# Scores stored with the keys outside, the gates' exponential emitted later, and new stage slots ahead of the seven-product step

## The chip, the core and the metric

The kernel runs on one core of a Trainium2 chip. The time is the device time of one execution in microseconds (us). The engines of the core work in parallel and each runs its own instructions in order: PE (TensorE, matrix products), DVE (VectorE), ACT (ScalarE), POOL (GpSimd) and SP, which here only issues DMA transfers. ACT issues some DMA transfers too, in the same queue as its arithmetic, so an issue that has to wait holds up the arithmetic behind it.

## What is computed

Two branches over the same input x (2048 rows, 640 columns) are mixed by a gate per row, `g = sigmoid(sum(x * gate_w))`:

```python
a = einsum("bsd,ed->bse", x, dft_hid_re);  b = einsum("bsd,ed->bse", x, dft_hid_im)
A = einsum("ts,bse->bte", dft_seq_re, a) - einsum("ts,bse->bte", dft_seq_im, b)
q = einsum("nd,dhc->nhc", x, w_q)                       # 32 heads, two halves of 128
s1 = einsum("nhd,ed->nhe", q[..., :128], k1);  s2 = einsum("nhd,ed->nhe", q[..., 128:], k2)   # 16 keys each
# the two best keys of s1 and of s2, the two best of their four sums -> two experts of 256 per head
gate = softmax(top_s);  act = gelu(x . u[expert]);  B = sum(gate * act * v[expert])
out = g * A + (1 - g) * B
```

The part that matters here is the choice of the keys: for each of the 2048 rows there are 32 heads times two halves = 64 groups of 16 scores, and in each group the largest and the second largest score and their places are needed.

## The kernel before

**Products.** Every float32 operand is split into a high and a low part (`split`, L129 on ACT for the high part, L130 on POOL or DVE for the low part), and each product is made of three (`mm3`, L134 to L136). A 128x512 result stays in one of eight PSUM banks (`b0` to `b7`).

**Stages.** The sequence transform comes in pieces `n = 0 .. NPC-1`, one 128x512 block of the transform matrix each (`wf`, split into `WS`, three pieces ahead of PE). Sixteen pieces make a chunk of 512 output columns in banks 0 to 4; at the chunk's end ACT copies the five banks into the five slots of the stage tile `ST` (L253), DVE multiplies them by the gate row (`gate_piece`, L225), and ACT issues their stores to DRAM (`store_piece`, L232). The stage slots are handed out in turn, 0 to 4. From piece `N0` (31) to `N1` (71) PE alternates the pieces with the score products: `score_half(i, a)` makes the scores of rows tile `i` (of 16), half `a` of the 64 groups, in bank 5 or 6 in turn, and ACT copies them into the tile `sc` (L585); `sc` has two slots, so tile `i + 2` needs the slot of tile `i`. From piece `Q0` (80) a chunk pair is made with seven products in place of eight (units `a11`, `s1`, `a12`, ...): `quad_step`. Its results rest in the same `ST` slots: `c22` in slots 0 and 1, `c` in slots 2 and 3, `w` in slot 4. After the eight steps of `a11`, `q_post` copies bank 0 into `w` (L304) and banks 5 and 6 into `c` (L275). The first `a12` step adds its last product onto bank 0, so PE needs the copy into `w` first; banks 5 and 6 are next written by unit `s2`, 16 steps later.

**The choice of keys** (`topk`, DVE only, once per rows tile): the largest of each group (L598, a reduction over 16), a comparison of all 1024 scores with it (L600), a product with a table of places (L602), the largest of that (L604, a reduction over 16), a comparison of the table with that place (L607), the chosen score pushed far down (L609), and the first four again. `sc` and the work tile `ew` are stored `[64 groups, 16 keys]`, the keys inside. After four rows tiles, `gates(b)` forms the four sums and picks two on DVE, ACT takes an exponential (L624), and DVE makes the two gate factors (L640 to L647). `rows(b)` then issues, per rows tile, three transposing DMAs on SP (L659) into `rt`, and ACT or (for the last four tiles) POOL copies `rt` into the table `rows` (L667, L665; steps of 8 elements in the output). `experts()` compares these rows on DVE (L808 to L810), PE sums them (L836), ACT copies the sums out (L817) and issues their stores (`gd<-cd`, L823).

**Order.** The order on every engine is the order of the calls in the program; nothing moves them later. The background work (`topk`, `gates`, `rows`, `experts`) is a list of generators in `Pump`. After every `mm3` the pump is told 0.68 us, runs generators up to a share of that time, and counts down the functions given to `space`, each of which is called a stated number of pump microseconds after the one before it. `at(n, f)` calls `f` after piece `n`.

**DMA counters.** All DMAs of SP and ACT take one of eight completion counters (`DMAHW0` to `DMAHW7`) in turn, in program order across both queues. Before an issue, its engine waits for the DMA that had the same counter before, so an issue on ACT can wait for a transfer of SP's queue.

Of the kernel before, what the change touches and what calls it, by code (L numbers as in the profile page):

```python
# [8 lines left out]
F32 = mybir.dt.float32  # L9
# [88 lines left out]
def gated_mix_kernel(ctx: ExitStack, tc: tile.TileContext, xT, xn, dreT, dimT, wsre, wsim, wq, kT, uT, vv, gw, out):  # L98
# [25 lines left out]
    def stage():  # L124
        return ST[:, rotate("st", 5)]
# [110 lines left out]
    def seq_piece(n):  # L236
# [11 lines left out]
        for d in ((4, 0, 1, 2, 3) if n == NPC - 1 else range(KD)):  # L248
            ds = slice(d * P, (d + 1) * P)
            mm3(banks[d], X[s][:, 0, ds], X[s][:, 1, ds], h, l, s == 0, s == NT - 1)  # L250
            if s == NT - 1:
                staged[w * NC + c, d] = f = stage()
                nc.scalar.activation(f, banks[d], AF.Copy)  # L253
            run_bg(0.68)
# [47 lines left out]
    def q_post(n, what):  # L302
        if what == "a11":
            nc.scalar.activation(qres["w"], qrole["W"], AF.Copy)  # L304
            q_copy("c", "X")
        elif what == "s1":
# [65 lines left out]
    for q, n in ((0, NT), (1, 2 * NT), (2, 3 * NT), (3, 4 * NT), (6, Q0), (7, NPC)):  # L372
        at(n + (2 if q == 0 else -5 if q == 6 else -2 if q > 1 else -1), load_row, q)
        at(n + (7 if q == 0 else 0), gate_piece, q)
        at(n + (8 if q == 0 else 4 if q == 6 else 1), store_piece, q)

# [176 lines left out]
    for n in range(N0):  # L553
# [11 lines left out]
    pools.append(p2)  # L565
    SC = pa.tile([P, 2, HH, E], F32, name="sc", tag="A")
    EW = pa.tile([P, 2, HH, E], F16, name="ew", tag="B")
    eq, wtab = EW[:, 0], EW[:, 1]
    nc.gpsimd.iota(wtab, pattern=[[0, HH], [-1, E]], base=E, channel_multiplier=0,
                   allow_small_or_imprecise_dtypes=True)  # L570
# [3 lines left out]
    def score_half(i, a):  # L574
# [7 lines left out]
        for k in range(KD):  # L582
            mm3(ps, xh[:, k, :], xl[:, k, :], WH[:, k, c], WL[:, k, c], k == 0, k == KD - 1)
            run_bg(0.68)
        nc.scalar.activation(scs[i].rearrange("p h e -> p (h e)")[:, c], ps, AF.Copy)  # L585
        if a == 1:
            picks(i, scs.pop(i))

    def topk(i, sc):
# [5 lines left out]
        for s in range(2):  # L595
            m = mm[:, s, ib, :]
            r = rr[:, s, ib, :]
            nc.vector.tensor_reduce(m, sc, op=OP.max, axis=AX.X)  # L598
            yield 1.22
            nc.vector.tensor_tensor(eq, sc, m[:, :, None].to_broadcast([P, HH, E]), op=OP.is_equal)  # L600
            yield 1.31
            nc.vector.tensor_tensor(eq, eq, wtab, op=OP.mult)  # L602
            yield 1.0
            nc.vector.tensor_reduce(r, eq, op=OP.max, axis=AX.X)  # L604
            yield 1.22
            if s == 0:
                nc.vector.tensor_tensor(eq, wtab, r[:, :, None].to_broadcast([P, HH, E]), op=OP.is_equal)  # L607
                yield 1.22
                nc.vector.scalar_tensor_tensor(sc, eq, FAR, sc, op0=OP.mult, op1=OP.add)  # L609
                yield 1.44  # L610

    def gates(b):
# [10 lines left out]
        nc.vector.tensor_sub(c[:, 1], c[:, 1], c[:, 0])  # L623
        nc.scalar.activation(c[:, 2], c[:, 1], AF.Exp)  # L624
        yield 1.2
# [12 lines left out]
        yield 1.3  # L638

        nc.vector.tensor_scalar(c[:, 1], c[:, 2], 1.0, None, op0=OP.add)  # L640
        nc.vector.reciprocal(c[:, 0], c[:, 1])
# [6 lines left out]
        gated[b] = (rp, gs)  # L648
        yield 1.5

    def rows(b):
# [26 lines left out]
        for a in range(NB + 1):  # L678
            bg.space(lambda a=a: step(a), 16.0 if a == 0 and b == NT // NB - 1 else 5.0 if b == NT // NB - 1 else 8.0)
        yield 0.0  # L680
# [5 lines left out]
    def picks(i, sc):  # L686
        bg.add(done(i, topk(i, sc)))
        if i % NB == NB - 1:
            bg.add(gates(i // NB))
        elif i and i % NB == 0:  # L690
            bg.add(rows(i // NB - 1))
        if i == NT - 1:
            bg.add(rows(NT // NB - 1))

# [535 lines left out]
```

## Time and profile before

| what | value |
|---|---|
| median of three runs | 785.89 us (785.76 to 787.21) |
| the profiled execution: its own time, and its span | 786.74 us, 785.0 us |
| PE busy | 762.9 us (97% of the span) |
| DVE busy | 579.9 us (74%), nearly all the time from 190 to 440 us |
| ACT busy | 302.2 us (38%) |
| POOL busy | 342.2 us (44%) |
| pieces with scores (the score stage) | about 150 to 420 us |
| start of the seven-product step | about 459 us |

A row of the timeline gives the start, the length, the engine, the line and the tiles, and in brackets how long the engine stood idle before and what ended that. `ACTq` and `SPq` rows are DMA issues. A row of groups gives the count, the busy time, the mean length in ns, and the idle time ahead.

### The profile page before, as it was taken

Reading aid. Unit: us, or ns where it says so; the run is one execution under the profiler, and the core shown is the slowest. Engines: PE = TensorE matmul, PEld = TensorE weight load, DVE = VectorE, ACT = ScalarE, POOL = GpSimd, SP = SyncE. Lnnn points to the kernel's source line nnn. Section 1 sums busy time; section 2 is a strip of 40 time slices with the busy share of each in tenths; the row PEclk is TensorE's granted clock in tenths of the full one; section 3 lists DMA queues with packets and bytes.
Section 4 is the critical chain, followed back from the end, with each engine's and each line's share of the span. In section 5 each row is a group of like instructions: output and inputs, shape, how many; then the busy total and the mean of one; then the engine's idle time right before and its main releaser. Section 6 shows DMA issues by size and latency. Waiting matters only on the chain.

```text
span 785.0 us, 12383 instructions
## 1 busy us (share of the span) xinstructions
PE 762.9 (97%) x4568; PEld 612.4 (78%) x4568; DVE 579.9 (74%) x676; ACT 302.2 (38%) x505; POOL 342.2 (44%) x239
## 2 busy tenths in 40 slices
PE   9999999999999999998999996999999999999997
PEld 6777677888888788886888774877777887788886
DVE  7651121398999999999999984888888768748761
ACT  5344323322315243344334442444334442543351
POOL 4532224466756476476654042000002466567253
PEclk9999999999999999999999997999999999999999
DMA  9966986645445665456645487798857486676411
GB/s 343 375 247 187 300 336 220 213 155 194 144 167 165 213 197 205 156 158 220 228 146 183 161 244 230 230 292 267 271 149 235 154 292 218 198 257 216 127 61 68
DMA packets 115180, 165.29 MB, mean 211 GB/s; under 512 B 35760, under 2 KB 51248, under 8 KB 115120
## 3 DMA queue, kind: packets, MB, share of 16 engines
q1 hardware_dynamic: 85648, 144.69, 56.1%
q10 hardware_dynamic: 29472, 19.81, 8.0%
q8 instruction: 36, 0.59, 0.3%
q14 instruction: 24, 0.20, 0.1%
HBM read 126.17 MB, written 36.71 MB: 208 GB/s over the span
## 4 chain that ended last, share of the span: by engine, by line
PE 52%; DVE 27%; DMA 9%; POOL 4%; issue 3%; SPq 2%; ACT 2%; ACTq 0%; DVEq 0%; POOLq 0%
PE b L134 17%; PE b L135 16%; PE b L136 16%; DVE ew L600 3%; DVE rr L604 3%; DVE mm L598 3%; DVE ew L602 3%; POOL WS L130 2%; PE b L479 2%; DVE ew L607 2%; DMA wf<-in_wsim 2%; DVE ST L225 2%; DVE sc L609 2%; DVE WS L130 2%; DMA wq<-in_wq 1%
## 5 line engine op out<-in xcount | busy, mean ns | idle before, releaser
L134 PE MATMUL b<-WS,X 128*128 128x512 f32 x555 | 221.2, 399 | 10.8 <-ACT ST L304 7.5
L135 PE MATMUL b<-WS,X 128*128 128x512 f32 x555 | 217.9, 393 | 1.6 <-DVE WS L130 1.6
L136 PE MATMUL b<-WS,X 128*128 128x512 f32 x555 | 217.1, 391 | 0.0
L130 POOL TENSOR_TENSOR WS<-wf,WS 128x512 fp32r<-128x512 f32 x72 | 109.4, 1525 | 134.1 <-ACT WS L129 125.7
L134 PEld LDWEIGHTS b<-WS,X 128*128 128x128 f32 x555 | 104.8, 189 | 42.5 <-ACT ST L304 8.0
L129 ACT ACTIVATE WS<-wf 128x512 fp32r<-128x512 f32 x152 | 94.5, 632 | 95.1 <-PE b L136 41.1
L135 PEld LDWEIGHTS b<-WS,X 128*128 128x128 f32 x555 | 104.9, 189 | 23.9 <-DVE WS L130 3.4
L136 PEld LDWEIGHTS b<-WS,X 128*128 128x128 f32 x555 | 104.8, 189 | 22.5
L130 DVE TENSOR_TENSOR WS<-wf,WS 128x512 fp32r<-128x512 f32 x80 | 54.3, 702 | 27.0 <-ACT WS L129 26.9
L130 POOL TENSOR_TENSOR WS<-ra,WS 128x512 fp32r<-128x512 f32 x40 | 59.2, 1497 | 15.1 <-ACT WS L129 14.4
L585 ACT ACTIVATE sc<-b 128x512 f32<-128x512 f32 x32 | 19.5, 608 | 119.5 <-PE b L136 112.0
L130 POOL TENSOR_TENSOR ts<-tf,ts 128x256 fp32r<-128x256 f32 x12 | 11.0, 939 | 122.5 <-ACT ts L129 122.5
L136 PE MATMUL b<-WU,xl 128*128 128x512 f32 x160 | 62.4, 390 | 0.4 <-POOL xl L130 0.4
L134 PE MATMUL b<-WU,xh 128*128 128x512 f32 x160 | 62.3, 389 | 0.0
L135 PE MATMUL b<-WU,xh 128*128 128x512 f32 x160 | 62.3, 389 | 0.0
L129 ACT ACTIVATE WS<-ra 128x512 fp32r<-128x512 f32 x56 | 34.7, 630 | 53.6 <-PE b L136 27.9
L130 POOL TENSOR_TENSOR WP<-ra,WP 128x512 fp32r<-128x512 f32 x20 | 32.2, 1625 | 47.1 <-ACT WP L129 44.1
L494 DVE TENSOR_TENSOR WU<-b,WU 128x512 fp32r<-128x512 f32 (+1 forms) x16 | 7.8, 490 | 59.4 <-ACT WU L493 59.4
L600 DVE TENSOR_TENSOR ew<-sc,mm 128x1024 f16<-128x1024 f32 x32 | 50.6, 1583 | 1.1
L598 DVE TENSOR_REDUCE mm<-sc 128x64 f32<-128x1024 f32 x32 | 38.9, 1215 | 13.7 <-ACT sc L585 13.2
L983 DVE TENSOR_TENSOR ra<-ra 128x512 f32<-128x512 f32 x48 | 43.9, 963 | 4.1 <-POOL WP L130 3.0
L604 DVE TENSOR_REDUCE rr<-ew 128x64 f16<-128x1024 f16 x32 | 39.0, 1219 | 1.0
(156 smaller groups left out, 1433.6 us busy)
## 6 DMA issues: line engine op xcount, KB each, us to landing
wq<-in_wq SPq DMA_DIRECT2D x32, 640.0 KB, 6.6
ra<-pd SPq DMA_DIRECT2D x70, 256.0 KB, 4.2
wf<-in_wsre SPq DMA_DIRECT2D x63, 256.0 KB, 5.0
wf<-in_wsim SPq DMA_DIRECT2D x56, 256.0 KB, 4.2
sa<-in_wsim SPq DMA_DIRECT2D x32, 256.0 KB, 3.0
sd<-sa SPq DMA_DIRECT2D x32, 256.0 KB, 3.1
wf<-sd SPq DMA_DIRECT2D x32, 256.0 KB, 4.4
tq<-td SPq DMA_DIRECT2D x32, 256.0 KB, 4.1
```

What stands on the lines that cost most here:

```text
L129: nc.scalar.activation(h, f, AF.Copy)
L130: eng.tensor_sub(l, f, h.bitcast(F32))
L134: nc.tensor.matmul(o, wh, ah, start=first, stop=False, skip_group_check=more)
L135: nc.tensor.matmul(o, wh, al, start=False, stop=False, skip_group_check=more)
L136: nc.tensor.matmul(o, wl, ah, start=False, stop=last, skip_group_check=more)
L225: nc.vector.scalar_tensor_tensor(f, f, -1.0 if w else 1.0, g, op0=OP.mult, op1=OP.mult)
L585: nc.scalar.activation(scs[i].rearrange("p h e -> p (h e)")[:, c], ps, AF.Copy)
L598: nc.vector.tensor_reduce(m, sc, op=OP.max, axis=AX.X)
L600: nc.vector.tensor_tensor(eq, sc, m[:, :, None].to_broadcast([P, HH, E]), op=OP.is_equal)
L602: nc.vector.tensor_tensor(eq, eq, wtab, op=OP.mult)
L604: nc.vector.tensor_reduce(r, eq, op=OP.max, axis=AX.X)
L983: nc.vector.tensor_add(take((b, o, k)) if f is not None else raw[b, o, k], raw[b, o, k] if f is None else f, raw[b, what, k])
```

## The change

Three things are changed, and nothing of what is computed.

1. **Layout.** `sc` and `ew` are `[16 keys, 64 groups]`, so neighbouring elements are neighbouring groups, and the keys of a group lie 64 elements apart. The comparisons and products (L600, L602, L607, L609, in the changed file L603, L605, L610, L612) read and write in storage order, and the broadcast operand (`m`, `r`) is now read as 64 neighbouring values, 16 times over, in place of each value 16 times in a row. The two reductions read each group in steps of 64 elements (256 bytes in `sc`, 128 bytes in `ew`). The copy of the scores (L585, now L588) reads its bank in order and writes in steps of 64 elements.
2. **The exponential.** `gates` ends before it; a function `second` is given to `space` with 8.0, which emits the exponential (now L643) and adds `factors`, which holds the rest of the gates and then runs `rows`. `rows` is no longer added by `picks`, and the waits between its steps for the last four tiles are 8.0 and then 5.0 in place of 16.0 and then 5.0.
3. **The stage slots.** At the last piece ahead of `Q0` the turn is set so that the five results go to slots 4, 0, 1, 2, 3; their stores are issued one piece earlier (`Q0 + 3`); and the copy of banks 5 and 6 into `c` comes four pieces after the copy into `w`.

```diff
@@ seq_piece
             if s == NT - 1:
+                if n == Q0 - 1 and d == 0:
+                    turn["st"] = 3
                 staged[w * NC + c, d] = f = stage()
@@ q_post
         if what == "a11":
             nc.scalar.activation(qres["w"], qrole["W"], AF.Copy)
-            q_copy("c", "X")
+            at(n + 4, q_copy, "c", "X")
@@ the table of gate and store pieces
-        at(n + (8 if q == 0 else 4 if q == 6 else 1), store_piece, q)
+        at(n + (8 if q == 0 else 3 if q == 6 else 1), store_piece, q)
@@ tiles
-    SC = pa.tile([P, 2, HH, E], F32, name="sc", tag="A")
-    EW = pa.tile([P, 2, HH, E], F16, name="ew", tag="B")
+    SC = pa.tile([P, 2, E, HH], F32, name="sc", tag="A")
+    EW = pa.tile([P, 2, E, HH], F16, name="ew", tag="B")
-    nc.gpsimd.iota(wtab, pattern=[[0, HH], [-1, E]], base=E, channel_multiplier=0,
+    nc.gpsimd.iota(wtab, pattern=[[-1, E], [0, HH]], base=E, channel_multiplier=0,
@@ score_half
-        nc.scalar.activation(scs[i].rearrange("p h e -> p (h e)")[:, c], ps, AF.Copy)
+        h = slice(a * TC // E, (a + 1) * TC // E)
+        nc.scalar.activation(scs[i][:, :, h].rearrange("p e h -> p h e"), ps.rearrange("p (h e) -> p h e", e=E), AF.Copy)
@@ topk
-            nc.vector.tensor_reduce(m, sc, op=OP.max, axis=AX.X)
+            nc.vector.tensor_reduce(m, sc.rearrange("p e h -> p h e"), op=OP.max, axis=AX.X)
-            nc.vector.tensor_tensor(eq, sc, m[:, :, None].to_broadcast([P, HH, E]), op=OP.is_equal)
+            nc.vector.tensor_tensor(eq, sc, m[:, None].to_broadcast([P, E, HH]), op=OP.is_equal)
-            nc.vector.tensor_reduce(r, eq, op=OP.max, axis=AX.X)
+            nc.vector.tensor_reduce(r, eq.rearrange("p e h -> p h e"), op=OP.max, axis=AX.X)
-                nc.vector.tensor_tensor(eq, wtab, r[:, :, None].to_broadcast([P, HH, E]), op=OP.is_equal)
-                yield 1.22
+                nc.vector.tensor_tensor(eq, wtab, r[:, None].to_broadcast([P, E, HH]), op=OP.is_equal)
+                yield 0.9
@@ gates
-        nc.scalar.activation(c[:, 2], c[:, 1], AF.Exp)
+        def second():
+            nc.scalar.activation(c[:, 2], c[:, 1], AF.Exp)
+            bg.add(factors(b, c, rp))
+
+        bg.space(second, 8.0)
+
+    def factors(b, c, rp):
         nc.vector.tensor_scalar(c[:, 1], c[:, 2], 1.0, None, op0=OP.add)
...
         gated[b] = (rp, gs)
         yield 1.5
+        yield from rows(b)
@@ rows
-            bg.space(lambda a=a: step(a), 16.0 if a == 0 and b == NT // NB - 1 else 5.0 if b == NT // NB - 1 else 8.0)
+            bg.space(lambda a=a: step(a), 5.0 if a and b == NT // NB - 1 else 8.0)
@@ picks
-        elif i and i % NB == 0:
-            bg.add(rows(i // NB - 1))
-        if i == NT - 1:
-            bg.add(rows(NT // NB - 1))
```

The order on ACT around the third exponential (score stage, piece 64, the end of chunk 3), with the counters that each instruction waits for. Before:

```order
L129 ACTIVATE WS<-wf 128x512 [waits PE_49]
L624 ACT_TABLE_LOAD
L624 ACTIVATE cc<-cc 128x128 [waits DVE_49]
L585 ACTIVATE sc<-b_2928 128x512 [waits PE_49]
L129 ACTIVATE WS<-wf 128x512 [waits DMAHW6_49]
L253 ACTIVATE ST<-b_2102 128x512 [waits PE_49]
L253 ACTIVATE ST<-b_2103 128x512 [waits PE_49]
```

And in the change:

```order
L588 ACTIVATE sc<-b_2929 128x32x16 [waits DVE_49,PE_49]
L129 ACTIVATE WS<-wf 128x512 [waits DMAHW6_49]
L255 ACTIVATE ST<-b_2102 128x512 [waits PE_49]
L255 ACTIVATE ST<-b_2103 128x512 [waits PE_49]
L255 ACTIVATE ST<-b_2104 128x512 [waits DMAHW0_49,PE_49,Pool_49]
L255 ACTIVATE ST<-b_2105 128x512 [waits DMAHW2_49,PE_49,Pool_49]
L255 ACTIVATE ST<-b_2106 128x512 [waits DMAHW5_49,DMAHW4_49,PE_49]
L588 ACTIVATE sc<-b_2996 128x32x16 [waits PE_49]
L129 ACTIVATE WS<-wf 128x512 [waits DMAHW4_49]
L643 ACT_TABLE_LOAD
L643 ACTIVATE cc<-cc 128x128 [waits DVE_49]
```

The exponential and its table load stood ahead of the chunk's five bank copies and now stand behind them, one score half later.

The order on ACT at the end of unit `a11` (the copy into `w`, L304, L306 in the change). Before:

```order
L817 ACTIVATE cd<-b_3913 128x32x16 [waits PE_49]
L823 DMA gd<-cd 1024x1x32 [waits DMAHW6_49,Activation_49]
L823 DMA gd<-cd 1024x1x32 [waits DMAHW1_49]
L304 ACTIVATE ST<-b_3768 128x512 [waits DMAHW7_49]
L275 ACTIVATE ST<-b_3769 128x512 [waits DMAHW0_49]
L275 ACTIVATE ST<-b_3770 128x512 [waits DMAHW2_49,PE_49]
L129 ACTIVATE WS<-wf 128x512 [waits DMAHW7_49,DVE_49]
```

And in the change:

```order
L823 ACTIVATE cd<-b_3913 128x32x16 [waits PE_49]
L829 DMA gd<-cd 1024x1x32 [waits DMAHW4_49,Activation_49]
L829 DMA gd<-cd 1024x1x32 [waits DMAHW6_49]
L306 ACTIVATE ST<-b_3768 128x512
L129 ACTIVATE WS<-wf 128x512 [waits DVE_49,PE_49]
```

The two stores of the experts' sums still stand ahead of the copy into `w`, with other counters; the copy waits for no transfer any more, and the copies into `c` have left this place. Whose transfers those counters belong to is seen on SP. Before, the third trio of transposes of the last four rows tiles stands like this (the last of the trio takes counter 6, the second `tq` load behind it counter 1):

```order
L659 DMA_TRANSPOSE rt<-rp 128x128 [waits DMAHW4_49,Pool_49]
L659 DMA_TRANSPOSE rt<-rp 128x128 [waits DMAHW5_49]
L659 DMA_TRANSPOSE rt<-gs 128x128 [waits DMAHW6_49]
L264 DMA tq<-td 128x512 [waits DMAHW7_49]
L188 DMA wf<-in_wsim 128x512 [waits DMAHW0_49,DVE_49]
L264 DMA tq<-td 128x512 [waits DMAHW1_49]
```

And in the change (the first `tq` load takes counter 4, the first transpose of the trio counter 6):

```order
L266 DMA tq<-td 128x512 [waits DMAHW4_49]
L188 DMA wf<-in_wsim 128x512 [waits DMAHW5_49,DVE_49]
L669 DMA_TRANSPOSE rt<-rp 128x128 [waits DMAHW6_49,Pool_49]
L669 DMA_TRANSPOSE rt<-rp 128x128 [waits DMAHW7_49]
L669 DMA_TRANSPOSE rt<-gs 128x128 [waits DMAHW0_49]
```

So the two stores waited for SP's queue up to the second `tq` load behind the third trio, and now wait for it up to the first transpose of that trio; two loads that stood behind the trio have moved ahead of it.

## The prediction, made before the changed kernel ran

> **What bounds the kernel now.** I read the page's shares first, then PE's own waits, then PE's timeline at the two longest of them, then what the engine that released PE was doing.
>
> ```profile
> PE 762.9 (97%) x4568; PEld 612.4 (78%) x4568; DVE 579.9 (74%) x676; ACT 302.2 (38%) x505; POOL 342.2 (44%) x239
> PE b L134 <- ACT ST L304: 7.5, 1, 7.5
> PE b L134 <- ACT ST L253: 2.7, 2, 2.4
> ```
>
> PE bounds the kernel: 762.9 of 785.0 us. No product is added or taken away, so a gain can only come out of the 22 us in which PE stands, and of what those stands cost behind them. Two single waits make up 10 us, and both are released by ACT. Around them PE's timeline reads (start, length):
>
> ```profile
> 364.29 0.39 PE L136 MATMUL b<-WU,xl 128*128 128x512 f32 x1
> 367.12 0.79 PE L134 MATMUL b<-WS,X 128*128 128x512 f32 x1 [2.44 <-ACT ST L253]
> 370.18 0.39 PE L135 MATMUL b<-WS,X 128*128 128x512 f32 x1
> ...
> 473.16 0.39 PE L135 MATMUL b<-WS,X 128*128 128x512 f32 x1
> 473.39 0.39 PE L136 MATMUL b<-WS,X 128*128 128x512 f32 x1
> 481.30 0.80 PE L134 MATMUL b<-WS,X 128*128 128x512 f32 x1 [7.53 <-ACT ST L304]
> 486.14 0.39 PE L136 MATMUL b<-WS,X 128*128 128x512 f32 x1
> ```
>
> A product starts 0.23 us after the one before it where PE runs freely (473.16, 473.39). At the first place the step from 364.29 to 367.12 is 2.60 us too long, and the 7 products from 367.12 to 370.18 take 3.06 us in place of 1.59: the products stay slow for a while after the stand. Together **4.1 us**. At the second, the step from 473.39 to 481.30 is 7.68 us too long, and the 11 products up to 486.14 take 4.84 us in place of 2.49. Together **10.0 us**. The granted clock in 481 to 486 us is 0.50:
>
> ```profile
> 481.00:486.00 5.00, 4.70 (x11) 3.74 (x12) 2.96 (x3) 3.23 (x7) 2.44 (x1) 0.50 0.78 181
> ```
>
> Why ACT was late at the first place: its exponential stood for DVE's sums, and the five bank copies that PE needed were queued behind it. At the second: the copy into `w` stood behind two stores, which waited for their counters.
>
> ```profile
> 365.27 0.31 ACT L624 ACTIVATE cc<-cc 128x128 f32<-128x128 f32 x1 [7.60 <-DVE cc L623]
> 366.48 2.54 ACT L253 ACTIVATE ST<-b 128x512 f32<-128x512 f32 x5
> ...
> 460.74 8.17 ACTq L232 DMA_DIRECT2D pd<-ST  x5
> 469.04 1.67 ACT L129 ACTIVATE WS<-wf 128x512 fp32r<-128x512 f32 x3 [7.68 <-DMA rt<-rp]
> 470.62 0.57 ACT L817 ACTIVATE cd<-b 128x512 f32<-128x512 f32 x1
> 477.43 3.17 ACTq L823 DMA_DIRECT2D gd<-cd  x2
> 480.65 0.60 ACT L304 ACTIVATE ST<-b 128x512 f32<-128x512 f32 x1 [9.46 <-DMA tq<-td]
> ```
>
> The second bound is near: DVE, in the score stage. Sum of nine stretches of 30 us from 170 to 440 us, and DVE's only wait for scores there:
>
> ```profile
> sum 270.00, PE 266.58 PEld 224.39 DVE 258.58 ACT 102.07 POOL 159.57; mean PE 29.62 PEld 24.93 DVE 28.73 ACT 11.34 POOL 17.73
> DVE mm L598 <- ACT sc L585: 3.0, 1, 3.0
> ```
>
> DVE works 258.6 of 270 us, so work added to it there has nowhere to go.
>
> **The change, part by part.** *The exponential* (three edits of `gates`, `rows`, `picks`). Nothing is added. It moves behind the five copies, some 36 products or 8 us of PE time later, so DVE's sums, which came 7.60 us after ACT stood ready, are done or nearly done when ACT gets there. The copies then run when PE ends the chunk, and the first stand goes: **-4.1 us**. If the cover failed, ACT would stand there again, but with a score copy and not a bank copy behind it, and PE has a second score bank. The row transposes follow up to some 30 products later than before; their table is read only in the later `experts`.
>
> *The stage slots.* Store order and slots change, so `w` (slot 4) is stored first; its copy waits for no transfer now. What is left ahead of it are the two `gd<-cd` stores. SP's rows there:
>
> ```profile
> 467.40 0.58 SPq L264 DMA_DIRECT2D tq<-td  x1
> ...
> 469.66 3.41 SPq L659 DMA_TRANSPOSE rt<-rp  x2
> ...
> 475.63 0.43 SPq L264 DMA_DIRECT2D tq<-td  x1
> 475.63 4.41 DMA tq<-td
> 480.06 0.54 ACTq L823
> rt<-rp SPq DMA_TRANSPOSE x32, 2.7
> ```
>
> Before, the second store had to wait for the load issued at 475.63, which landed at 480.04. Now it waits for the first transpose of that trio. That one started at 469.66; two loads more stand ahead of it, at 0.57 us each (467.40 to 469.66 for four), which gives 470.8, and 2.7 us to land give 473.5. The store's issue takes 0.5 and the copy 0.6, so PE gets its bank at about 474.7 where it wants it at 473.6: a stand of 1.1 us. A stand that short left no slow products behind it at 461 us:
>
> ```profile
> 461.99 0.50 PE L135 MATMUL b<-WS,X 128*128 128x512 f32 x1 [1.07 <-DVE WS L130]
> 462.33 0.40 PE L136 MATMUL b<-WS,X 128*128 128x512 f32 x1
> ```
>
> So **-8.9 us**; between -10.0 (nothing left) and 0 (another late transfer takes the place). The five `pd<-ST` issues now wait for the first trio, not the second, which frees ACT's splits at 469.04 earlier; the splits were not late for PE even so. The copies into `c` cost the same 1.08 us four pieces later, and their banks are wanted 16 steps later.
>
> *The layout on DVE.* The rows of five of the six instructions, with the mean in ns and then the shortest, the middle and the longest of two of them:
>
> ```profile
> L598 DVE TENSOR_REDUCE mm<-sc 128x64 f32<-128x1024 f32 x32 | 38.9, 1215 | 13.7 <-ACT sc L585 13.2
> L600 DVE TENSOR_TENSOR ew<-sc,mm 128x1024 f16<-128x1024 f32 x32 | 50.6, 1583 | 1.1
> L602 DVE TENSOR_TENSOR ew<-ew 128x1024 f16<-128x1024 f16 x32 | 34.6, 1081 | 1.1
> L604 DVE TENSOR_REDUCE rr<-ew 128x64 f16<-128x1024 f16 x32 | 39.0, 1219 | 1.0
> L607 DVE TENSOR_TENSOR ew<-ew,rr 128x1024 f16<-128x1024 f16 x16 | 25.0, 1562 | 0.5
> L602 DVE TENSOR_TENSOR ew<-ew x32: 684/693/1947, 161.5 to 433.7; 128x1024 f16<-128x1024 f16 x32
> L607 DVE TENSOR_TENSOR ew<-ew,rr x16: 1225/1227/2349, 163.8 to 427.7; 128x1024 f16<-128x1024 f16 x16
> ```
>
> L607 becomes what L602 is already, two f16 operands in storage order, and so takes 0.69 to 1.08 us: 16 x (1.56 - 1.08) = 7.7 us saved, up to 14. L600 has an f32 operand; its shortest run (1224) equals a reduction, so I give it nothing. The two reductions now read in steps of 64 elements, which no DVE row shows. Two rows of ACT are nearest, a strided read (L817, its bank in steps of 32 elements) and a strided write (L667, steps of 8), beside the same engine's copy in order (L585):
>
> ```profile
> L817 ACT ACTIVATE cd<-b x16: 575/598/600, 448.3 to 601.1; 128x512 f32<-128x512 f32 x16
> L667 ACT ACTIVATE rows<-rt 128x384 f16<-128x384 f16 x12 | 23.4, 1954 | 8.0 <-DMA rt<-gs 7.7 <-issue 0.3
> L585 ACT ACTIVATE sc<-b 128x512 f32<-128x512 f32 x32 | 19.5, 608 | 119.5 <-PE b L136 112.0 <-DVE ew L607 7.4
> ```
>
> The strided read costs nothing (598 for 512 elements), the strided write takes 5.1 ns an element against 1.2. A reduction only reads with steps, so I take L817's answer: 1.22 us as before. The other end, L667's 4.3-fold, would be 5.2 us each, four more on 64 instructions; the rival below takes the first step towards it.
>
> [...]
>
> With reductions unchanged DVE wins 8 to 14 us in a stage where PE rarely waits for it: at 310 to 322 us the topk of a tile starts 12 us after its scores, and PE runs on.
>
> ```profile
> 309.84 0.60 ACT L585 ACTIVATE sc<-b 128x512 f32<-128x512 f32 x1 [5.68 <-PE b L136]
> 321.91 1.21 DVE L598 TENSOR_REDUCE mm<-sc 128x64 f32<-128x1024 f32 x1
> ```
>
> I count **-0.5 us** for that, out of the few stands of 0.4 to 1.2 us between 270 and 462 us.
>
> *The layout on ACT.* The score copy writes with steps; L667 gives 512 x 5.1 = 2.6 us against 0.6, 32 times 2.0 = 64 us, and its lower bound is nothing. Even the 64 lie beside other work: ACT works 102 of those 270 us, PE has the other score bank for 6.8 us, the splits are three pieces ahead, and DVE has its lag. Where DVE waits (3.0 us, once) it waits 2 longer. I count **+0.3 us**.
>
> The sum on the profiled execution's own 786.74 us (span 785.0 and 1.7 around it): -4.1 - 8.9 - 0.5 + 0.3 = -13.2, so 773.5. That execution lies 0.85 above the median, inside the three runs' spread of 1.45, so I say **773.0 us**.
>
> **The rivals.** *Strided reductions cost.* If a strided element takes DVE two steps in place of one, a reduction grows by up to 1.2 us: 64 x 1.2 = 78 us. L607 gives 8 back. The four comparing instructions now run 37 us above their shortest (L600 0.36 x 32, L602 0.40 x 32, L607 0.34 x 16, L609 0.48 x 16), while reductions always take 1.22, so POOL, which shares the stage, does its work under longer reductions, and I give half of the 37 back. That leaves 52 us. A topk that starts 12 us late and takes 13 ends some 2 us before the slot is wanted again (two tiles of 17 us less one half), and PE's second score bank and the pieces split ahead give about 10 more: 12 us are free. Behind piece 71 DVE makes PE's splits too, behind its own backlog. So PE stands 40 us more, against the forecast's 773: about **813 us**. The sign turns once a reduction takes some 0.8 us more. For it: DVE's 96% and L667. Against it: L817.
>
> *The wait moves.* `w`'s copy is late all the same, because another transfer ahead of the stores lands late (4.4 us for a `tq` load as against 2.7 for a transpose, and a trio that starts late behind its buffers). Then the second stand stays near 7 us and only the first is gone: **782 us**. For it: eight counters in turn tie ACT to SP's queue everywhere. Against it: the transfer waited for is three issues earlier.
>
> *The gain is eaten.* The longer score copies on ACT delay the bank copies at three chunk ends and the splits behind them, with a slow clock after each stand of 2.4 us or more: 3 x 4 = 12 us, **786 us**. For it: the stand at 364 us arose in just this way. Against it: ACT is ahead of PE by a score half there.
>
> **How the numbers follow.** Forecast 0.53, the wait moves 0.12, the gain is eaten 0.07, strided reductions 0.28. The forecast's own range is 770 to 778. Below 770 I leave 0.05. The reductions' case lies by the same sum at 780 where each takes 0.7 us more and at 831 with 1.5; above 815 I leave 0.12. So the range is 770 to 815. This kernel's measurement tells 0.2%, 1.6 us, from no change. Faster: the first two cases and a little of the reductions' one, 0.67; same 0.07; slower 0.26.
>
> **What would show it.** Right: no wait of PE for the copy into `w` above 2 us and none for the bank copies at piece 64; the exponentials' idle time (30.9 us now) under 8; reductions at 1.22 us; L610 under 1.1. Wrong: reductions above 2 us with PE waiting for score copies or for DVE's splits between 190 and 460 us; or a wait near 7 us left at 474 us. The score copy at 0.6 or at 2.6 us tells only how ACT writes.

## The result: 2.8% slower, and the profile after

The change takes 808.37 us (median; 807.33 to 809.63) against 785.83 us before in the same comparison (785.74 to 787.21): a ratio of **1.028, 95% interval 1.0265 to 1.0302**. The forecast, 773.0 us and faster, is wrong in its sign. The time lies in the range because of the first rival, strided reductions, which put it at 813.

The profiled execution has a span of 806.5 us. Its busy times, and the rows by line of the instructions whose layout changed (count, busy time, mean in ns, idle time ahead):

```profile
PE 769.8 (95%) x4568; PEld 615.1 (76%) x4568; DVE 609.9 (76%) x676; ACT 316.7 (39%) x505; POOL 335.9 (42%) x239
L607 DVE TENSOR_REDUCE rr<-ew 128x64 f16<-128x1024 f16 x32 | 65.6, 2051 | 1.0
L601 DVE TENSOR_REDUCE mm<-sc 128x64 f32<-128x1024 f32 x32 | 63.9, 1996 | 11.2 <-ACT sc L588 10.7
L610 DVE TENSOR_TENSOR ew<-ew,rr 128x1024 f16<-128x1024 f16 x16 | 13.4, 837 | 0.5
L588 ACT ACTIVATE sc<-b 128x512 f32<-128x512 f32 x32 | 36.3, 1135 | 113.8 <-PE b L136 105.3 <-DMA pd<-ST 8.4
```

The two reductions went from 1.22 us to 2.05 and 2.00, **51.6 us more** on the engine that the prediction had called the second bound. L610 fell from 1.56 to 0.84 us (11.6 us less, inside the predicted 7.7 to 14). The score copy on ACT rose from 0.61 to 1.13 us. DVE's stretches of the score stage, ten of 30 us from 170 to 470 us, are now 98% full, and PE is idle for 24 of the 300 (before, 3.4 of 270):

```profile
sum 300.00, PE 275.95 PEld 228.37 DVE 294.02 ACT 118.20 POOL 157.27; mean PE 27.59 PEld 22.84 DVE 29.40 ACT 11.82 POOL 15.73
```

PE's longest waits (us in total, times, longest):

```profile
PE b L134 <- ACT xh L129: 10.9, 4, 7.0
PE b L135 <- DVE WS L130: 6.4, 3, 3.7
PE b L134 <- ACT ST L306: 4.8, 1, 4.8
PE b L136 <- POOL xl L130: 4.3, 5, 1.0
PE b L134 <- ACT sc L588: 2.6, 1, 2.6
```

The longest kind is new: the splits of `xh` (the x of a pair of rows tiles, for the score products) on ACT. What held them at the longest one, in the timeline of DVE, SP, ACT and PE:

```profile
347.39 0.68 DVE L729 TENSOR_TENSOR sa<-sa 128x512 f32<-128x512 f32 x1
348.10 2.48 SPq L745 DMA_DIRECT2D sd<-sa  x3
355.49 0.52 SPq L761 DMA_DIRECT2D sa<-in_wsim  x1
360.05 0.33 SPq L767 DMA_DIRECT2D sd<-sa  x1
362.90 1.22 SPq L669 DMA_TRANSPOSE rt<-gs  x1
364.85 1.32 SPq L721 DMA_DIRECT2D sa<-in_wsim  x3
367.06 1.04 ACTq L712 DMA_DIRECT2D actd<-ST  x2
368.15 1.36 ACT L129 ACTIVATE xh<-xf 128x640 fp32r<-128x640 f32 x2 [9.16 <-DMA sa<-in_wsim]
368.94 0.80 PE L134 MATMUL b<-WU,xh 128*128 128x512 f32 x1 [7.02 <-ACT xh L129]
```

DVE also makes sums (`sa`) that the seven-product step will need. Behind longer reductions they came late; SP's stores of them (`sd<-sa`) and the transposes and loads behind those came late; ACT's stores of the activations (`actd<-ST`, L712) take the same eight counters, so they waited for SP's load of `sa`; and the splits of `xh`, queued behind these stores, came 7 us too late for PE. SP's waits for DVE's sums are the trace of it, 37.3 us for the first of them (L729) from 170 to 470 us. Before, there was no such wait for the first sum and one of 0.4 us for the second. In the change, then before:

```profile
SPq L745 <- DVE sa L729: 37.3, 6, 8.2
SPq L739 <- DVE sa L724: 0.4, 1, 0.4
```

Of the two stands that were to go, the one at the bank copies of piece 64 is gone (the 0.3 us that PE still waits for such copies lie at 70 us), and the one at `w` is 4.8 us, not 1.1. The exponentials' idle time is 2.9 us, under the predicted 8.

### The profile page after: what moved, and what is told of

It reads as the page before. It is cut to its first block, busy times and chain, and to the rows that moved or that the text cites. A ratio compares the mean times of both kernels' runs of the same rounds, so it can differ in the third digit from the quotient of the medians.

```text
span 806.5 us, 12390 instructions
## 1 busy us (share of the span) xinstructions
PE 769.8 (95%) x4568; PEld 615.1 (76%) x4568; DVE 609.9 (76%) x676; ACT 316.7 (39%) x505; POOL 335.9 (42%) x239
## 4 chain that ended last, share of the span: by engine, by line
PE 47%; DVE 39%; DMA 5%; issue 4%; POOL 1%; ACT 1%; SPq 1%; ACTq 0%; DVEq 0%; POOLq 0%
PE b L134 14%; PE b L135 14%; PE b L136 14%; DVE mm L601 7%; DVE rr L607 7%; DVE ew L603 5%; DVE ew L605 4%; DVE sc L612 3%; PE b L481 2%; DVE ST L225 2%; DMA ra<-pd 2%; DVE ew L610 2%; DVE ra L989 1%; DVE WS L130 1%; DMA rt<-rp 1%
## 5 line engine op out<-in xcount | busy, mean ns | idle before, releaser
L130 POOL TENSOR_TENSOR WS<-wf,WS 128x512 fp32r<-128x512 f32 x72 | 107.4, 1497 | 115.1 <-ACT WS L129 108.8
L588 ACT ACTIVATE sc<-b 128x512 f32<-128x512 f32 x32 | 36.3, 1135 | 113.8 <-PE b L136 105.3
L134 PE MATMUL b<-WU,xh 128*128 128x512 f32 x160 | 63.8, 399 | 10.9 <-ACT xh L129 10.9
L601 DVE TENSOR_REDUCE mm<-sc 128x64 f32<-128x1024 f32 x32 | 63.9, 1996 | 11.2 <-ACT sc L588 10.7
L607 DVE TENSOR_REDUCE rr<-ew 128x64 f16<-128x1024 f16 x32 | 65.6, 2051 | 1.0
L135 PE MATMUL b<-WU,xh 128*128 128x512 f32 x160 | 63.2, 395 | 0.0
L603 DVE TENSOR_TENSOR ew<-sc,mm 128x1024 f16<-128x1024 f32 x32 | 47.4, 1480 | 1.1
```

Of the source, the lines that this page charges most:

```text
L130: eng.tensor_sub(l, f, h.bitcast(F32))
L134: nc.tensor.matmul(o, wh, ah, start=first, stop=False, skip_group_check=more)
L135: nc.tensor.matmul(o, wh, al, start=False, stop=False, skip_group_check=more)
L588: nc.scalar.activation(scs[i][:, :, h].rearrange("p e h -> p h e"), ps.rearrange("p (h e) -> p h e", e=E), AF.Copy)
L601: nc.vector.tensor_reduce(m, sc.rearrange("p e h -> p h e"), op=OP.max, axis=AX.X)
L603: nc.vector.tensor_tensor(eq, sc, m[:, None].to_broadcast([P, E, HH]), op=OP.is_equal)
```

## The experiments

Each time is compared with runs of the kernel before on the same chip (784.3 to 785.7 us).

### The edits apart

`layout_only` is the kernel before with the layout edit alone, `old_layout` the change with that edit undone.

> The kernel before with the layout edit alone. Theory A: the layout costs 35 us on a kernel without the other two gains, so 815 to 822 us. Rival B (the three edits make the loss together): well below 808, near 790.

> The change without its layout edit: keys inside again, the exponential apart and the new stage slots kept. Theory A (the reductions' longer rows, 2.00 and 2.05 us in place of 1.22, are the whole loss): reductions back at 1.22 us, DVE about 52 us less busy than in the change, and the prediction's two other terms show: 773 to 776 us. Rival B (the later exponential or the new slots bring part of the loss, for the waits of PE for a split late behind a store's DMA): stays above 786.

`layout_only`: 813.1 us, ratio **1.039** (1.034 to 1.044), by the ratio 30.5 us slower; the time lies 2 us under theory A's range. `old_layout`: 788.1 us, ratio **1.004** (1.002 to 1.006), by the ratio 3.2 us slower where 11 faster were expected. So the layout makes the whole loss, but rival B's other half also holds: the other two edits did not bring their 13 us. In PE's row of `layout_only` the bank copies ahead of which the exponential stands cost more than before:

```profile
L134 PE MATMUL b<-WS,X 128*128 128x512 f32 x555 | 221.5, 399 | 18.9 <-ACT ST L253 8.2 <-ACT ST L304 7.1 <-ACT WS L129 2.3
```

By the ratios the whole change loses 22.2 us, 8.3 less than the layout alone. Which of the other two edits saves that, no run separates. In the two traces the stand of 8.0 us at the bank copies is gone in the change, but PE's waits for `xh` are 10.9 us there and 2.3 in `layout_only`, and the stand at `w` is 4.8 us there and 7.1 in `layout_only`.

### DVE's time, or the steps?

`nine_keys` changes the two reductions of the change, and leaves out seven keys (the other reduction is shortened in the same way):

```diff
+KR = 9
-            nc.vector.tensor_reduce(m, sc.rearrange("p e h -> p h e"), op=OP.max, axis=AX.X)
+            nc.vector.tensor_reduce(m, sc[:, :KR].rearrange("p e h -> p h e"), op=OP.max, axis=AX.X)
```

> The change with both reductions over the first 9 of 16 keys (the last seven keys are left out of the choice), still in steps of 64 elements, so that a reduction takes about 1.2 us again; the score copy still writes 16 keys with steps (1.13 us on ACT). Theory A: DVE's time is the whole cause, so 773 to 778 us. Rival C (the strided score copy on ACT, or DVE and ACT getting into each other's way on the tile with steps, costs PE time by itself): over 785.

`more_dve` adds to the kernel before, ahead of each reduction, one in storage order (here the one ahead of the first; `xm` is read by nobody):

```diff
+XG = 40
+            nc.vector.tensor_reduce(xm, sc[:, :XG], op=OP.max, axis=AX.X)
             nc.vector.tensor_reduce(m, sc, op=OP.max, axis=AX.X)
```

> The kernel before with one more reduction in storage order, over 40 of the 64 groups, ahead of each of the 64 reductions; its result goes to a tile that nobody reads. That is 64 times some 0.8 us on DVE, as much as the steps of 64 cost in the change, without any steps and without the other edits. Theory A (only the time on DVE counts, 12 us of it are free): 35 to 45 us more than before, 820 to 830 us. Rival D (the loss is particular to accesses with steps): within 5 us of before.

`nine_keys`: 782.1 us, ratio 0.996 (0.994 to 0.998). `more_dve`: 826.1 us, ratio 1.053 (1.051 to 1.055). Rows of `nine_keys`, then of `more_dve`:

```profile
L602 DVE TENSOR_REDUCE mm<-sc 128x64 f32<-128x576 f32 x32 | 38.5, 1203 | 21.3 <-ACT sc L589 20.8
L589 ACT ACTIVATE sc<-b 128x512 f32<-128x512 f32 x32 | 35.9, 1123 | 126.1 <-PE b L137 126.1
```

```profile
L608 DVE TENSOR_REDUCE xq<-ew 128x40 f16<-128x640 f16 x32 | 26.2, 819 | 1.0
L601 DVE TENSOR_REDUCE xm<-sc 128x40 f32<-128x640 f32 x32 | 26.1, 815 | 10.7 <-ACT sc L588 10.2
```

With steps of 64 but 1.2 us a reduction the loss is gone, though ACT's copies still take 1.12 us; with 52.3 us more on DVE and no step at all it is there. So **DVE's time is the cause**, and rivals C and D fall. `nine_keys` lies 4 us above theory A's range, but that range still held the 13 us of the other two edits: against `old_layout`, which has the same two, it is 6 us faster. `pairs_all` below, with the same two edits, the same time for a reduction and ACT's copies at 0.65 us, came to the same ratio, 0.996, so the longer copies cost nothing that shows.

The runs also give the free lag. In `more_dve` the 52.3 us of new instructions cost 41.6, so some 11 are free. In `layout_only` the reductions took 51.5 us more, L608 (L610 of the change) 11.3 less and the other three 2.9 less; that is 37.3, which cost 30.5, so some 7 are free. By DVE's whole busy time (579.9 us before, 612.4 in `layout_only`, 627.2 in `more_dve`) only 2 and 6 are. The prediction's rival had 12.

### Which steps cost

`steps` holds only such instructions, four of each, with no product beside them (lines between the two places are left out):

```diff
+        for step in (1, 2, 4, 8, 16, 32, 64, 65, 66):
+            v = groups(src[dt], step)
...
+            for m in range(4):
+                nc.vector.tensor_reduce(d, v, op=OP.max, axis=AX.X)
```

> Only single instructions, nothing of the computation (the output is zeros): reductions of 64 groups of 16 in steps of 1, 2, 4, 8, 16, 32, 64, 65 and 66 elements, in f32 and f16, four of each; the halving maximum of 512 and 512 elements in storage order; score copies of 512 elements on ACT with steps of 1 to 64 elements in the output, f32 and f16. No other engine works beside them. Theory A1 (any step over one element costs DVE the same): 1.22 us at step 1 and about 2.0 us at every other step. Theory A2 (the step of 256 bytes, a power of two, is the cause): the cost grows towards 64, and 65 and 66 are back near 1.2 us. Theory A3 (the 2.0 us come from DVE and POOL working side by side): 1.22 us at every step here. For ACT: 0.6 us at step 1 and 1.1 us in f32 at step 64; whether f16 in steps of 8 takes the 5 us per thousand elements of the copy into rows.

Two steps at a time alternate, four instructions each. DVE's busy time in five stretches: f32 steps 1 and 2; 4 and 8; 64 and 65; then f16 steps 2 and 4; 8 and 16. Start:end, length, busy time with the count (one that a boundary cuts is counted twice), then clock and transfers:

```profile
5.70:14.71 9.01, 8.96 (x9) 1.00 1.02 421
14.71:29.95 15.24, 15.24 (x10) 1.00 0.10 44
44.34:59.18 14.84, 14.84 (x10) 1.00 0.00 0
71.49:80.50 9.01, 9.01 (x9) 1.00 0.00 0
80.50:95.46 14.96, 14.96 (x10) 1.00 0.00 0
```

Eight reductions take 9.01 us, 1.13 from start to start, at f32 steps 1 and 2 and at f16 steps 2 and 4; they take 14.1 to 15.2, 1.77 to 1.91 each, at f32 steps 4 and more and f16 steps 8 and more, at 65 and 66 as at 64. None of the three theories had it: what counts is the step **in bytes, up to 8 free and from 16 on some 1.65 times the time**. POOL does nothing in these stretches. ACT's copies run beside DVE up to 78.7 us, but in the last stretch, f16 steps 8 and 16, no other engine works and the longer time is there all the same.

ACT's score copies, four each, beside DVE's reductions, at f32 steps 1, 2 and 4, then f16 steps 1 and 8:

```profile
3.60:5.99 2.39, 2.28 (x4) 1.00 0.94 384
5.99:8.48 2.49, 2.40 (x5) 1.00 1.02 421
8.48:12.68 4.20, 4.10 (x5) 1.00 1.00 414
29.52:31.95 2.43, 2.33 (x6) 1.00 0.00 0
39.91:49.45 9.54, 9.45 (x5) 1.00 0.00 0
```

ACT's copy takes 0.60 us in order and 0.62 and 1.05 at steps of 2 and 4 in f32; in f16 it takes 0.61 in order and 2.39 at step 8, which is 16 bytes. The prediction took the f16 row (5.1 ns an element) for an f32 write.

### A layout that keeps the gain

`pairs` is the kernel before with the keys 2 elements apart. Of its diff (`ew`, the table, the score copy and the other instructions are changed alike):

```diff
-    SC = pa.tile([P, 2, HH, E], F32, name="sc", tag="A")
+    SC = pa.tile([P, 2, HH // 2, E, 2], F32, name="sc", tag="A")
-            nc.vector.tensor_reduce(m, sc, op=OP.max, axis=AX.X)
+            nc.vector.tensor_reduce(pair(m), sc.rearrange("p b e g -> p b g e"), op=OP.max, axis=AX.X)
-                nc.vector.tensor_tensor(eq, wtab, r[:, :, None].to_broadcast([P, HH, E]), op=OP.is_equal)
+                nc.vector.tensor_tensor(eq, wtab, pair(r)[:, :, None].to_broadcast([P, HH // 2, E, 2]), op=OP.is_equal)
```

> The kernel before with another layout: two groups side by side, so that a group's keys lie 2 elements apart; nothing else is changed. Theory A (a step of 4 elements or more is what made the reductions longer; at step 2 the single instructions took 1.21 us and the score copy 0.62): reductions at 1.22 us and score copies at 0.62 to 0.65 us, the comparison with the place faster than its 1.56 us if neighbouring pairs are enough for it, and the time at or under that of before, 779 to 785. Rival B (a layout with the keys apart costs in the kernel whatever the step): over 795.

> The change with the keys 2 elements apart in place of 64, its other two edits kept. Theory A, and the other two edits together worth 3.5 us of loss as in the run without the layout edit: about 3 us above the run with pairs alone, 782 to 788. By the prediction's two other terms it would be 13 us below it, about 770.

`pairs_all` is the change with this layout in place of its own. `pairs`: 781.5 us, ratio **0.993** (0.991 to 0.996), faster than both kernels. `pairs_all`: 782.2 us, 0.996 (0.994 to 0.998); it is not shown to be slower than `pairs`, as the intervals overlap. Rows of `pairs`:

```profile
L602 DVE TENSOR_REDUCE mm<-sc 128x64 f32<-128x1024 f32 x32 | 38.9, 1216 | 16.4 <-ACT sc L586 15.8
L611 DVE TENSOR_TENSOR ew<-ew,rr 128x1024 f16<-128x1024 f16 x16 | 13.8, 866 | 0.6
L586 ACT ACTIVATE sc<-b 128x512 f32<-128x512 f32 x32 | 21.0, 657 | 117.7 <-PE b L136 111.0 <-DVE ST L225 6.7
```

The faster comparison that the layout was predicted to bring is there (0.87 us) and nothing of the reductions' cost. For the time it is worth more than the 0.5 us that the prediction gave it: by the ratios 5.2 us here, and 6.3 us from `old_layout` to `pairs_all`.

`tree` replaces each strided reduction of the change by four maxima of halves:

```diff
+        for n in (8, 4, 2, 1):
+            u = f[:, :n] if n > 1 else o[:, None]
+            nc.vector.tensor_tensor(u, t[:, :n], t[:, n:2 * n], op=OP.max)
+            t = f
```

> The change with each reduction replaced by four halving maxima in storage order (512, 256, 128 and 64 results); the keys stay 64 elements apart. From the single instructions (0.68 us in f32 and 0.42 us in f16 for 512 results) a halving set takes about 1.5 us in f32 and 0.95 us in f16, 2.4 together where the strided pair takes 4.05 and the old pair 2.44. Theory A (DVE's time alone decides): DVE as busy as in the kernel before less the 11 us of the faster comparison, so 780 to 788. Rival C (the score copy of 1.13 us on ACT counts too): over 790.

It took 831.8 us (four of five executions 829.8 to 834.5, one 870.4), ratio 1.057 (1.053 to 1.061): my price was wrong. Two of its eight rows:

```profile
L595 DVE TENSOR_TENSOR ew<-ew 128x512 f16<-128x512 f16 x32 | 21.4, 668 | 1.0
L595 DVE TENSOR_TENSOR mm<-ew 128x64 f32<-128x64 f32 x32 | 13.1, 409 | 1.1
```

512 results in f16 took 0.67 us here against 0.42 alone, and even 64 results took 0.41, with a shortest of 0.22. All eight kinds sum to 154.5 us, against 129.5 for the strided reductions and 77.9 before. Eight short instructions with two inputs are no cheap reduction. Their lengths spread: the maximum with 64 results in f32 had a median of 0.23 us and a longest of 1.58. In the kernel before, the product L602, which has two inputs too, took 0.68 to 0.69 us in each of the 15 instances that had no POOL instruction beside them, and 0.69 to 1.95 (median 1.66) in the 15 that had one for half their time or more, while all 64 reductions took 1.20 to 1.22, with POOL beside them or not.

### Why the other two edits gave nothing

> The kernel before with the exponential's edit alone (and the rows behind it, as in the change). By the prediction's first term: the first stand (2.60 us and the slow products behind it) is gone, 4.1 us less than before. Rival (the later row transposes fall among the loads of the seven-product step and cost SP's queue as much): the time within 1.6 us of before or above it, with the stand at the copy into w at 7 us or more.

> The kernel before with the new stage slots alone. By the prediction's second term: 8.9 us less than before, the copy into w about 1 us late. Rival (the wait moves: with these edits alone the second store ahead of the copy has the counter of a load of tq that is issued behind the trio of transposes): a stand of 6 to 8 us is left at the copy into w, the time within 3 us of before.

`exp_only`: 786.1 us, ratio 1.001 (1.000 to 1.003). `slots_only`: 786.8 us, 1.003 (1.001 to 1.004). In their times both rivals hold, and that of `slots_only` in its wait too; in `exp_only` the stand at `w` is 5.3 us and not 7 or more.

The first thing that the prediction missed shows in `slots_only`. Up to 455 us its instructions are those of the kernel before, in the same order on every engine, and yet PE has no stand at the bank copies of piece 64 (the 0.2 us below lie at 70 us). ACT's exponential stood for DVE just as long as before, 7.61 us, but was over 2.1 us earlier, and PE came there 0.9 us later, so the bank copies began before PE wanted them, at 365.39:

```profile
PE b L134 <- ACT ST L255: 0.2, 1, 0.2
363.20 0.31 ACT L626 ACTIVATE cc<-cc 128x128 f32<-128x128 f32 x1 [7.61 <-DVE cc L625]
364.42 2.54 ACT L255 ACTIVATE ST<-b 128x512 f32<-128x512 f32 x5
```

So the stand of 4.1 us that the exponential's edit was to remove is not in every execution. In `pairs`, which leaves the exponential where it was, it is absent as well. How often it comes, two traces of one order can't tell.

In `exp_only` the stand is gone too, but PE waits 2.9 us for `xh` at 283 and 356 us. ACT there:

```profile
283.27 0.97 ACTq L709 DMA_DIRECT2D actd<-ST  x2
284.28 1.36 ACT L129 ACTIVATE xh<-xf 128x640 fp32r<-128x640 f32 x2 [7.04 <-DMA sa<-in_wsim]
```

It is the chain seen in the change: the rows' transposes moved along with the exponential, to a place between the transfers of the sums, and the stores that wait for those hold `xh`. The first of the two waits is in all three traces with this order up to there (`exp_only`, `old_layout`, `stores_sp`), the second in two. In `slots_only` the stand at `w` is 8.6 us: ACT's copy came free with a `tq` load that SP had issued behind a trio of transposes. In `old_layout` both edits change the order, and SP's rows show what the prediction's 470.8 became:

```profile
464.89 0.32 SPq L266 DMA_DIRECT2D tq<-td  x1
466.01 2.37 SPq L668 DMA_TRANSPOSE rt<-rp  x2
468.42 2.59 SPq L668 DMA_TRANSPOSE rt<-gs  x1
474.10 2.37 SPq L668 DMA_TRANSPOSE rt<-rp  x2
```

The trio that the second store waits for starts at 474.1: SP stood 3.1 us for a `tq` load (ahead of 464.89), and the trio of 466.01 took 1.4 us longer than the next one, waiting at its third transpose.

I tried to free each link. `exp_rows` is `exp_only` with the first transposes of three batches emitted earlier (first diff line pair). `exp_act` (from `exp_only`), `act_sp` (from the change) and `pairs_act` (from `pairs`) move the stores of the activations from ACT's queue to SP's (second pair). `stores_sp` (from `old_layout`) moves those of `cd` (third pair, its last lines left out), and `pairs_sp` (from `pairs`) both:

```diff
-            bg.space(lambda a=a: step(a), 5.0 if a and b == NT // NB - 1 else 8.0)
+            bg.space(lambda a=a: step(a), 5.0 if a and b == NT // NB - 1 else 8.0 if a or b == NT // NB - 1 else 0.5)
-            nc.scalar.dma_start(actd[n][:, 2 * p * P:2 * (p + 1) * P], act[:, n])
+            nc.sync.dma_start(actd[n][:, 2 * p * P:2 * (p + 1) * P], act[:, n])
-                    nc.scalar.dma_start(gd[g, n, :, :, :, :, w].rearrange("s j e f m -> (s j e) f m"),
+                    nc.sync.dma_start(gd[g, n, :, :, :, :, w].rearrange("s j e f m -> (s j e) f m"),
```

> The kernel with the exponential's edit alone, and the row transposes of the first three batches 7.5 pump microseconds earlier, so that none stands between the loads and stores of the sums (sd, sa) on SP's queue. Theory T (with the exponential's edit alone the first stand went, but transposes that stand among those transfers made the splits of xT late, 2.9 us of waits with the slow products behind): PE's waits for xh at 283 and 356 us go, and the time is 2 to 4 us under that of the exponential's edit alone, 782 to 784. Rival U (those waits come from DVE's later sums, not from SP's order): the waits for xh stay, 786 again.

> The kernel with the exponential's edit alone, and the stores of the activations issued on SP. Theory X: PE's waits for xh at 283 and 356 us (2.9 us and the slow products behind them) go, and the exponential's gain shows: 780 to 783 where before is at 785. Rival U (nothing hangs on those stores): within 1.6 us of the exponential's edit alone, 785 to 788.

> The change without its layout edit, and with the stores of cd issued on SP in place of ACT, so that nothing that waits for a transfer stands ahead of the copy into w on ACT. Theory W (in the change the copy into w is late because SP's transfers ahead of the two stores are late, and that stand is the second term that did not come): PE's stand for the copy into w goes from 7.2 us to under 1.5, and the time is 7 to 10 us below the same kernel with the stores on ACT, 778 to 781. Rival V (SP, which issues every load, comes late by the stores' own waits, and PE stands for a load or a split in their place): 786 to 790, with a new wait of PE behind SP's queue.

> The change whole (strided reductions too), with the stores of the activations (actd) issued on SP in place of ACT, so that the splits of xh on ACT don't stand behind them. Theory X (DVE's late sums hold SP, SP's late loads hold these stores by their counter, and the stores hold the splits that PE needs): PE's waits for xh, 10.9 us in four, go to under 3, and with the slow products behind them the time falls by 10 to 15 us, to 793 to 800. Rival Y (DVE's backlog reaches PE anyway, by the score tile's slots and by DVE's own splits behind piece 71): those waits move to score copies and DVE's splits, 804 to 812.

- `exp_rows`: 790.2 us, 1.006 (1.004 to 1.008), 4 us above what either theory said. The waits for `xh` did not go; they moved with the transposes, to 249 and 324 us. Theory T's gain fell.
- `exp_act`: 784.0 us, 1.000 (0.998 to 1.002). No wait of PE for `xh` is left, but 5.5 us for DVE's splits, nearly all between 423 and 443 us, stand in their place. The intervals of this and of `exp_only` overlap, so a gain isn't shown.
- `stores_sp`: 786.1 us, 1.002 (1.000 to 1.004). The stand at `w` is gone altogether, but SP issues without a break from 475 to 491 us and its loads come late: rival V, in PE's row

```profile
493.10 0.77 PE L135 MATMUL b<-WS,X 128*128 128x512 f32 x1 [3.41 <-DVE WS L130]
```

- `act_sp`: 806.7 us, 1.028 (1.026 to 1.031), as slow as the change. PE's waits for `xh` fell from 10.9 to 0.9 us as theory X says, and nothing was won, as rival Y says:

```profile
PE b L135 <- DVE WS L130: 6.8, 2, 4.3
PE b L136 <- POOL xl L130: 6.6, 3, 3.1
PE b L134 <- ACT sc L588: 3.8, 1, 3.8
```

So the stores are one way by which DVE's lag reaches PE, and not the only one. Where DVE has room, the same move is worth more than I expected:

> Pairs (keys 2 elements apart, the other edits left out) with the stores of the activations issued on SP. In the trace of pairs PE did not wait for xh at all, so nothing is to be had by theory X: within 1.6 us of pairs alone, 780 to 783.

> Pairs with the stores of the activations and those of cd on SP, so that the copy into w on ACT waits for no transfer. Theory W: PE's stand of 8.1 us for that copy goes with its slow products, 772 to 775. Rival V (SP's queue is full there: transposes at 1.2 us each and loads back to back, and with the stores on it the loads for DVE's splits come late): a stand of 3 to 5 us for DVE's splits some 15 us later, 778 to 782.

`pairs_act`: 775.7 us, ratio **0.989** (0.987 to 0.990), the best kernel of this study with `pairs_sp`, 775.6 us, 0.988 (0.986 to 0.990). The interval of `pairs_act` lies wholly below that of `pairs`, though PE had no wait for `xh` in that trace. Of the 6.3 us between the two profiled spans (779.7 and 773.4), 1.2 are a score copy's at 273 us and 0.5 POOL's `xl` at 285 us, both gone, and 1.5 are the stand at `w`, 6.6 us and not 8.1. The rest of the difference I can't place. In `pairs_sp` the stand at `w` became one of 3.0 us for ACT's splits some 13 us later, between theory W and rival V; the stores of `cd` on SP bring nothing beyond `pairs_act`.

## Why the prediction was wrong, step by step

- **The layout on DVE, -0.5 us: the step that failed.** It took a reduction with steps as 1.22 us "as before" from L817, ACT's strided read, and set aside the other end. L817 reads PSUM and on another engine; nothing in it speaks for DVE reading SBUF. Measured: 2.00 and 2.05 us, 51.6 us in all, and by the ratio 30.5 us of time by that edit alone. The term was wrong on the gain's side too: DVE's relief without the cost is worth 5 to 6 us (`pairs`, `pairs_all`) and not 0.5. Not every step costs: f32 keys 8 bytes apart ran as fast as adjacent ones (1.13 us from start to start in `steps`). Of two ends, I chose by the nearest row in kind of access and not in engine and memory, and so left the rival 0.28.
- **The rival's own sum** (813; the change took 808.4, and the layout alone 813.1) was right in mechanism and near in size. Reductions grew by 0.81 us and not 1.2, 52 and not 78. L610's 11.6 was put at 8. The 18 us of relief at POOL did not come where it was put: the other three instructions (L603, L605, L612) together ran 1 us less. Some 9 us came at short instructions with two inputs in `gates` (`dp`, `rp`), which took up to 1.3 us beside POOL before and 0.2 to 0.3 without it in the change, and DVE's whole busy time rose by 30.0 us. The free lag of 12 was 2 to 11, by how it is counted. The rival's sign turned "once a reduction takes some 0.8 us more", and that is what came; by its own sum that would have been 787. So its 813 is partly luck: too long reductions made up for the relief and the lag that it counted and for the 13 us of the other two terms, which its 773 held as won.
- **The exponential, -4.1 us.** The stand went, as said; the time did not (+0.9 us by that edit alone, interval -0.3 to 2.0). Two steps failed. The term took a stand of one execution for the kernel's: with the same instructions, `slots_only` has none. And "The row transposes follow up to some 30 products later than before; their table is read only in the later `experts`" priced the data and not the queue: in SP's order the transposes hold the sums' transfers, whose counters hold ACT's stores, ahead of `xh`.
- **The stage slots, -8.9 us.** The failed step is "That one started at 469.66; two loads more stand ahead of it", which gave 470.8. It took SP's times from a trace in which the trios stood elsewhere. With both edits the trio started at 474.1 and PE stood 7.2 us. The rival "the wait moves", with 0.12, named this; its price of 782 is that of the profiled execution of `old_layout` (782.6), the fastest of ten, but the median was 788.1. Where the typical execution is 5 us longer no trace shows; that stays open.
- **The score copy, +0.3 us.** 1.13 us and not 0.6 or 2.6. That ACT has room for it is right: `nine_keys` carries 16 us of it and is not slower than before. So the rival "the gain is eaten" fell with it.

## What to carry to other kernels

Price a strided access from a row of the same engine, in the same memory and at the same step in bytes: here DVE's reductions read SBUF at steps up to 8 bytes for nothing (1.13 us for 1024 elements), so two neighbours side by side gave the whole gain of the new layout, and 16 bytes and more cost some 1.65 times the time (1.77 to 1.95 us). On an engine at 96% any such cost came out nearly whole here, less a lag of 2 to 11 us, whichever link carried it; freeing the link moved the wait for as long as DVE lagged (`act_sp`), and paid once DVE had room (`pairs_act`). And a stand that is taken from a queue shared by counters is counted as won only once the new order of every transfer ahead has been priced, and once a second trace of the same instructions has shown the stand.

## What was not expected of the hardware

- DVE's reduction: 1.13 us from start to start for 1024 elements at 4 and 8 bytes of step, 1.77 to 1.95 from 16 to 264 bytes, f32 and f16 alike; steps that are no power of two (65, 66) are no better than 64.
- ACT's strided write depends on the type: at 16 bytes of step 1.05 us for 512 elements in f32 and 2.39 us in f16.
- A two-input maximum with only 64 f32 results per partition took 0.22 to 1.58 us in `tree`. In the kernel before, a two-input product of 1024 f16 elements took 0.68 to 0.69 us where POOL did nothing beside it, and 0.69 to 1.95 us where POOL worked for half its time or more; reductions took 1.20 to 1.22 us, beside POOL or not.
